# A fused attention and spectral mixing kernel: PV with v stationary, shared diagonal score blocks, products in column tiles, transfers in pairs, and a new fixed order

## The chip, the cores and the metric

The kernel runs on one core of one Trainium2 chip. The metric is the device time of one launch in microseconds (us), as the median of several runs. Each run also lists the mean clock that was granted to TensorE. A run is called slow here when it lies over 1.5% above the fastest run of the same kernel, and slow runs are left out of ratios. PE is TensorE (PEld its weight loads), DVE is VectorE, ACT is ScalarE, POOL is GpSimd, SP is SyncE, which issues the transfers.

## The reference, cut to what matters

```python
def _A_ref(x, wq, wk, wv, wo, beta):          # x: 1 x 2048 x 640, 32 heads of 20, 4 segments of 512
    ...
    for s in range(N):
        qs, ks, vs = (q[:, :, s].copy(), k[:, :, s].copy(), v[:, :, s].copy())
        logits = jnp.einsum('bhqd,bhkd->bhqk', qs, ks) * scale + mask     # causal inside the segment
        p = _softmax(logits, axis=-1)
        a_dot = jnp.einsum('bhqk,bhkd->bhqd', p, vs)
        pq = phi(qs)
        num = jnp.einsum('bhld,bhde->bhle', pq, M)                         # memory of earlier segments
        den = jnp.einsum('bhld,bhd->bhl', pq, z)[..., None] + 1e-06
        outs.append(g * num / den + (1.0 - g) * a_dot)
        pk = phi(ks)
        M = M + jnp.einsum('bhld,bhle->bhde', pk, vs)
        ...
    return o @ wo
def _B_ref(x, w_r, w_i):                       # irfft2(rfft2(x) * W)
    ...
return g * a + (1 - g) * b                     # g = sigmoid((x * gate_w).sum(-1))
```

## The kernel before

All work is recorded as operations with their dependences, and a fixed list, found by a search ahead of time, says in which order each engine runs them. The kernel computes a schedule from that list with an assumed duration for every operation. The schedule sets only the buffers and semaphores; the engines then run strictly in that order. The part of it that concerns the port shared by VectorE and POOL:

```python
def one(self, eng, fn, n, r, w, prio, per=None, fix=None, name="", after=()):
    fix0, per0, late = {"act": (65, 0.833, 110.0), "dve": (67, 1.04, 68.0), "pool": (100, 0.945, 50.0)}[eng]
    ...                                                     # assumed ns: fix + per * n
def head(e):                                                # when could engine e start its next operation?
    ...
    if e == "dve" and o.lock:                               # o.lock: needs the shared port
        t = max(t, free["pool"])                            # assumed to go when POOL's present instruction ends
    elif e == "pool":
        t = max(t, port)
```

Attention works on 32 groups (4 segments, 8 groups of 4 heads). For one group, scores come from row-tiled products (4 heads at a time, 20 rows each), exponentials on ACT, masks on POOL, and PV products that hold the exponentials stationary and stream 21 columns of v (20 and one of ones, which gives the denominator):

```python
UNITS = (((0, (0,)),), ((0, (1, 3)),), ((1, (0,)),), ((0, (2,)), (1, (2,))), ((1, (1, 3)),))
# exp: one activation for each unit, 4 heads x 512 columns; 80 of 128x2048 in all
self.one("act", lambda e: e.activation(dst(), src(), ACT.Exp, scale=SC), 4 * width, ...)
for g, j in outs:                                            # 4 masks a group, one for each diagonal block of 128
    self.one("pool", lambda e, g=g, j=j: e.affine_select(
        self.ex.ap(self.exo(s, g) + JOFF[j], [1280, 4], [1, P]), ...,
        [[0, 4], [1, P]], ALU.is_ge, 0.0, base=0, channel_multiplier=-1), 512, ...)
# pv_group: 4 tiles of queries x 4 heads x (i + 1) blocks = 40 products of 21 columns
return (self.ps(bank, i * 88 + hh * VW, [1, DH + 1]), self.ex.ap(...), va.ap(..., [1, DH + 1]), jj == 0, jj == i, {})
# then on VectorE: denominator * gate, reciprocal, multiplication, and an addition of the memory part
```

The softmax here doesn't subtract the row's maximum and nothing guards it: scores larger than these inputs give would overflow.

## Time and profile before

| | before |
|---|---|
| median of its first three runs | 246.75 us (246.59 to 250.73) |
| span of the profiled run | 244.2 us, clock 1.00 |
| POOL busy | 132.2 us, of which masks 81.0 |
| time the kernel's own schedule gives for its order | 238.5 us |
| changes between whole-array, row-tiled and column-tiled products | 175 |

The prediction shows the page's busy line, stretches of time and the chain. A line of the view of waits tells which engine and tile waited for which, the time in all, how often, and the longest wait. Two waits of the kernel before, those for masks and for scores:

```profile
ACT ex L1137 <- PE psum L498: 14.8, 36, 1.4
...
PEld psum L498 <- POOL ex L1140: 1.4, 5, 0.4
```

PE waited only 1.4 us for masks.

### The profile page before, as it was taken

To read this page: it belongs to the slowest core of one execution; us is meant where nothing else is said; L and a number is where in the kernel's file an instruction comes from. 1 tells how busy PE (TensorE), PEld (TensorE's weight loads), DVE (VectorE), ACT (ScalarE), POOL (GpSimd) and SP (SyncE) were. 2 spreads that over 40 slices of the span, in tenths; PEclk is the share of its full clock that TensorE was granted. 3 is DMA by queue.
4 is the path that set the end of the run, shared out by engine and by line. 5 is a ranking of instruction groups with operands and counts; after the bars stand their busy time and mean duration, and the time that the engine had idled before them with its cause. 6 is when DMAs were issued, how large, how long until landed. Compare 5 with 4: busy or idle time off the path is not lost.

```text
span 244.2 us, 8905 instructions
## 1 busy us (share of the span) xinstructions
PE 233.1 (95%) x3702; PEld 139.8 (57%) x3702; DVE 198.8 (81%) x534; ACT 201.6 (83%) x204; POOL 132.2 (54%) x200
## 2 busy tenths in 40 slices
PE   7999999999999999999978999999899999999994
PEld 2344575557556457645644475645555667667683
DVE  1489997988999898979999999989999975643643
ACT  2088889999998998999987998888899878798820
POOL 8421861362648484455876385646567656407610
PEclk9999999999999999999999999999999999999999
DMA  7998866696493656756442546313442969586224
GB/s 185 328 358 231 218 172 169 205 182 172 138 192 92 168 128 150 226 164 200 109 104 71 144 137 182 94 59 111 118 100 71 203 144 97 79 123 116 77 62 131
DMA packets 55880, 36.71 MB, mean 150 GB/s; under 512 B 31792, under 2 KB 52128, under 8 KB 55840
## 3 DMA queue, kind: packets, MB, share of 16 engines
q1 hardware_dynamic: 54144, 35.32, 58.4%
q10 hardware_dynamic: 1696, 0.82, 1.2%
q8 instruction: 29, 0.48, 0.8%
q14 instruction: 11, 0.09, 0.1%
HBM read 19.86 MB, written 9.71 MB: 121 GB/s over the span
## 4 chain that ended last, share of the span: by engine, by line
PE 72%; DVE 16%; DMA 5%; ACT 4%; issue 2%; SPq 0%; DVEq 0%
PE psum L498 64%; PE psum L496 8%; DVE Pt L1287 4%; ACT ex L1137 3%; DMA xT<-in_A_x_dram 2%; DMA oT<-o_scr 2%; DVE Cp L509 2%; DVE Yt L1292 1%; DVE qu L509 1%; ACT et L1010 1%; DVE va L1045 1%; DVE Bt L509 1%; DVE on L1172 1%; DVE on L1177 0%; DVE phk L1021 0%
## 5 line engine op out<-in xcount | busy, mean ns | idle before, releaser
L1137 ACT ACTIVATE ex<-psum 128x2048 bf16<-128x2048 f32 x80 | 150.3, 1878 | 15.8 <-PE psum L498 14.8
L1140 POOL TENSOR_SCALAR_AFFINE_SELECT ex<-ex 128x512 bf16<-128x512 bf16 x128 | 81.0, 653 | 70.5 <-ACT ex L1137 66.7
L498 PEld LDWEIGHTS psum<-va,ex 128*128 128x128 bf16 x1280 | 39.0, 96 | 5.8 <-issue 1.3
L498 PE MATMUL psum<-va,ex 128*128 128x21 bf16 x1280 | 41.1, 172 | 0.1
L498 PE MATMUL psum<-xT,wk 128*128 128x512 bf16 (+1 forms) x140 | 33.3, 380 | 0.6 <-DMA xT<-in_A_x_dram 0.6
L498 PE MATMUL psum<-xT,wq 128*128 128x512 bf16 (+1 forms) x135 | 32.2, 380 | 1.2 <-DVE Bt L509 1.2
L498 PE MATMUL psum<-qp,kp 20*128 20x384 bf16 (+3 forms) x512 | 31.7, 301 | 0.7 <-ACT ex L1137 0.2
L498 PE MATMUL psum<-wv,xT 128*128 128x500 bf16 (+1 forms) x160 | 31.9, 300 | 0.2
L1287 DVE TENSOR_TENSOR Pt<-psum,Wt 128x642 bf16<-128x642 f32 x32 | 25.4, 822 | 0.8 <-PE psum L498 0.5
L496 PE MATMUL psum<-wo,oT 128*32 128x320 bf16 x480 | 23.0, 300 | 0.2 <-issue 0.2
L498 PEld LDWEIGHTS psum<-qp,kp 20*128 20x128 bf16 x512 | 9.0, 92 | 18.3 <-ACT ex L1137 9.6
L509 DVE CAST ot<-psum 128x320 bf16<-128x320 f32 x21 | 9.9, 489 | 11.6 <-PE psum L496 8.4
L498 PEld LDWEIGHTS psum<-wv,xT 128*128 128x128 bf16 x160 | 13.3, 97 | 10.0 <-DVE Ac L509 0.8
L498 PE MATMUL psum<-big,Ac 128*128 128x321 bf16 (+2 forms) x96 | 17.9, 256 | 0.8 <-DVE Cp L509 0.4
L1045 DVE TENSOR_TENSOR va<-psum,ebx 128x500 bf16<-128x500 f32 (+1 forms) x32 | 15.2, 484 | 3.5 <-PE psum L498 2.8
L498 PE MATMUL psum<-tt,Yt 128*128 128x256 bf16 (+1 forms) x96 | 17.0, 274 | 0.4 <-DVE qu L509 0.2
L1292 POOL TENSOR_TENSOR Yt<-Pt 128x321 bf16<-128x321 bf16 x18 | 13.4, 757 | 7.2 <-DVE Pt L1287 4.6
L509 DVE CAST qu<-psum 128x512 bf16<-128x512 f32 x20 | 13.6, 686 | 3.4 <-PE psum L498 3.2
L1333 DVE TENSOR_TENSOR G<-eo,psum 128x320 bf16<-128x320 f32 x32 | 14.9, 479 | 1.7 <-PE psum L496 0.9
L498 PEld LDWEIGHTS psum<-xT,wk 128*128 128x128 bf16 (+1 forms) x140 | 9.9, 97 | 10.9 <-issue 2.3
L1177 POOL TENSOR_TENSOR on<-on,mem 128x320 bf16<-128x320 bf16 x16 | 12.8, 806 | 5.8 <-DVE on L1172 5.8
L1172 DVE TENSOR_TENSOR on<-psum,rs 128x320 bf16<-128x320 f32 x32 | 15.3, 481 | 0.6
(85 smaller groups left out, 379.9 us busy)
## 6 DMA issues: line engine op xcount, KB each, us to landing
tt<-tab_tt SPq DMA_DIRECT2D x16, 256.0 KB, 3.3
xsb<-in_A_x_dram SPq DMA_DIRECT2D x8, 320.0 KB
kp<-k_scr SPq DMA_DIRECT2D x28, 80.0 KB
qp<-q_scr SPq DMA_DIRECT2D x28, 80.0 KB
o_scr<-on SPq DMA_DIRECT2D x12, 160.0 KB
out_dram<-ot SPq DMA_DIRECT2D x12, 160.0 KB
q_scr<-qu SPq DMA_DIRECT2D x6, 256.0 KB
k_scr<-qu SPq DMA_DIRECT2D x6, 256.0 KB, 3.9
```

The costliest lines, as they stand in the source:

```text
L496: h = e.matmul(dst, wt, r_, start=st, stop=sp_, **{**kw, "tile_position": (0, q), "skip_group_check": True})
L498: h = e.matmul(o_, l_, r_, start=st, stop=sp_, **kw)
L509: alts["dve"] = (lambda e: e.tensor_copy(dst(), src()), 67 + 1.04 * n, 68.0)
L1010: self.one("act", lambda e: e.activation(et.ap(0, [1, L]), qsl(), ACT.Exp), L, [qb], [b("et", pi_)], late, name="phi_exp")
L1045: self.one("dve", lambda e: e.tensor_tensor(va.ap(i * H * VW + h0 * VW, [VW, nh], [1, DH]), self.ps(bank, 0, [DH, nh], [1, DH]), self.ebx. ...
L1137: self.one("act", lambda e: e.activation(dst(), src(), ACT.Exp, scale=SC), 4 * width, [bank], [self.exb(s, g, j) for g, j in outs], prio - ...
L1140: self.one("pool", lambda e, g=g, j=j: e.affine_select(self.ex.ap(self.exo(s, g) + JOFF[j], [1280, 4], [1, P]), self.ex.ap(self.exo(s, g) ...
L1172: self.one("dve", lambda e, rs=rs, bank=bank, g=g: e.tensor_tensor(on.ap(80 * g, [D, 4], [DH, 4], [1, DH]), self.ps(bank, 0, [88, 4], [VW, ...
L1177: self.either(lambda e, g=g: e.tensor_tensor(on.ap(80 * g, [D, 4], [1, 80]), on.ap(80 * g, [D, 4], [1, 80]), self.mem.ap(80 * g, [D, 4], [ ...
L1287: self.one("dve", lambda e, ri=ri, Pt=Pt, Wt=Wt, bank=bank: e.tensor_tensor(Pt.ap(ri * 322, [644, 2], [1, KD]), self.ps(bank, 0, [0, 2], [ ...
L1292: fn = lambda e, r=r, a0=a0, a1=a1, op=op, Pt=Pt, Yt=Yt: e.tensor_tensor(Yt.ap(r * 322, [1, KD]), Pt.ap(a0 * 322, [1, KD]), Pt.ap(a1 * 322 ...
L1333: self.one("dve", lambda e, q=q, n2=n2, bank=bank, eo=eo: e.tensor_tensor(self.G.ap(n2 * D + 639 * q, [1 - 2 * q, 320]), eo.ap(q, [1, 320] ...
```

## The change

Its intent is to relieve PE, ACT and DVE: PV products that stream wide instead of 21 columns, score blocks shared around the diagonal so that fewer columns are exponentiated, and a normalisation that goes through a scratch round trip for three of four segments. Masks become seven a group (three of 512 columns in all, four of 256). Some products of v move into column tiles, transfers are merged, and the order is searched anew. The core of the diff:

```diff
-JOFF = (0, 512, 1024, 896)
+KPOS = (0, 256, 128, 384)
+VPIECES = ((0, 0, 512, 0), (1, 512, 384, 128), (2, 896, 192, 320), (2, 1088, 64, 256), (3, 1152, 64, 448), (3, 1216, 64, 384))
...
+    def pv_flipped(self, s, g):
+        for n_, (jj, o, n, q0) in enumerate(VPIECES):
+            for hh in range(4):
+                    return (self.ps(bank, q0, [1, n], p0=32 * hh, np_=32), va.ap(jj * H * VW + (4 * g + hh) * VW, [1, 32]),
+                            self.ex.ap(self.exo(s, g) + hh * 1280 + o, [1, n]), n_ == 0, n_ == 5,
+                            {"tile_position": (0, 32 * hh), "skip_group_check": True})
...
-        for g, j in outs:
-            self.one("pool", lambda e, g=g, j=j: e.affine_select(...), 512, [], [self.exb(s, g, j)], prio, name="mask")
+            if ks == "a":
+                self.mask(s, g, P, 512, 0, 64, ("a0",), ("m1",), prio, 64)
+                self.mask(s, g, P, 0, 0, P, (), ("a0",), prio, 0)
+            elif ks == "b":
+                self.mask(s, g, 64, 512, 512, P, (), ("b0", "m1"), prio, -64)
+                self.mask(s, g, P, e2, e2, 64, (), ("b0" if s < 3 else "b1",), prio, 64)
+            else:
+                self.mask(s, g, P, 1216 if s < 3 else 1152, sh, 64, ("c0",), ("m3",), prio, 64)
+                self.mask(s, g, P, sh, sh, 64, (), ("c0",), prio, 0)
+                self.mask(s, g, 64, 1152, 1152, P, (), ("c0", "m3"), prio, ...)
...
-    ORDER = (36, 0, 86, 56, 38, ...)        # one entry for each operation and its engine
+    ORDER = (34, 0, 100, 54, 82, ...)
```

## The prediction

> **What bounds the kernel now.** I read part 1 of the page first, then the busy time by stretch, then the timelines of PE and ACT.
>
> ```profile
> PE 233.1 (95%) x3702; PEld 139.8 (57%) x3702; DVE 198.8 (81%) x534; ACT 201.6 (83%) x204; POOL 132.2 (54%) x200
> ```
>
> PE looks like the one bound, but its records contain pipeline latency. The timeline of PE gives the real pace from the start of one row to the start of the next:
>
> ```profile
> 77.77 1.15 PE L498 MATMUL psum<-va,ex 128*128 128x21 bf16 x40
> ...
> 236.53 2.35 PE L498 MATMUL psum<-wo,oTl 128*32 128x320 bf16 x64
> 238.71 0.31 PE L498 MATMUL psum<-G,fbg 128*32 128x320 bf16 x4
> ```
>
> Forty PV products take 1.15 us with one latency of about 0.15 in it: 25 ns each, for 21 columns. The 64 column-tiled products take 238.71 - 236.53 = 2.18 us, so a set of four, 320 columns wide, takes 136 ns, or 0.425 ns a column. At such paces (216 ns for 512 columns, 136 for 321, never under 25) all products of the trace stream for 203 us. There are 175 changes between whole-array, row-tiled and column-tiled products; from start to start, less streaming, a change costs about 0.09 us into a row-tiled score set, 0.13 to 0.17 out of it, and 0.20 from column-tiled to whole. At 0.13 on average that is 23 us. So PE needs about 226 of the 237 us after the first input lands at 7 us.
>
> ```profile
> 40.00:60.00 20.00, 20.00 (x241) 11.32 (x234) 16.60 (x43) 19.12 (x24) 8.19 (x14) 1.00 0.74 187
> 140.00:160.00 20.00, 19.87 (x304) 12.53 (x304) 18.81 (x58) 18.57 (x18) 12.97 (x20) 1.00 0.51 142
> 180.00:200.00 20.00, 19.25 (x371) 11.92 (x371) 18.61 (x56) 17.71 (x16) 14.28 (x20) 1.00 0.61 133
> 200.00:220.00 20.00, 19.79 (x532) 12.98 (x524) 10.37 (x26) 16.46 (x16) 7.20 (x12) 1.00 0.81 107
> ```
>
> The columns are PE, PEld, DVE, ACT, POOL busy, clock, DMA. From 20 to 200 us ACT and DVE are each over 90% busy, beside PE: three engines bound the middle together. After 200 us DVE is half idle and PE works off inverse transforms and output products. The chain that ended last agrees:
>
> ```profile
> PE 72%; DVE 16%; DMA 5%; ACT 4%; issue 2%; SPq 0%; DVEq 0%
> ```
>
> The change must therefore relieve PE, ACT and DVE together, or it moves the bound to the one left out. The groups it touches:
>
> ```profile
> L1137 ACT ACTIVATE ex<-psum 128x2048 bf16<-128x2048 f32 x80 | 150.3, 1878 | 15.8 <-PE psum L498 14.8
> L1140 POOL TENSOR_SCALAR_AFFINE_SELECT ex<-ex 128x512 bf16<-128x512 bf16 x128 | 81.0, 653 | 70.5 <-ACT ex L1137 66.7 <-ACT gate L1043 3.5
> L1172 DVE TENSOR_TENSOR on<-psum,rs 128x320 bf16<-128x320 f32 x32 | 15.3, 481 | 0.6
> L1170 DVE RECIPROCAL rs<-rs 128x16 f32<-128x16 f32 x32 | 7.8, 244 | 0.5
> L1167 DVE TENSOR_TENSOR rs<-psum,gate 128x16 f32<-128x16 f32 x32 | 5.4, 168 | 7.1 <-PE psum L498 6.7
> ```
>
> **What the Trainium skill says.** "TensorE: Matmul & The Clock Gate", section "Wait — 56ns, not 53.3ns?": starts of matmuls never come closer than about 25 ns, however narrow they are. The trace agrees: 25 ns for 21 columns, where streaming alone would be 9. "TensorEngine Tiling (Array Packing)", section "When to Use Tiling", names the cure used here: where the moving side is narrow, swap the operands and tile by columns. Its section "Key Properties" says that a change of tiling mode drains the engine; the trace agrees, at 0.09 to 0.20 us a change. "Perfetto Trace Analysis", section "Identifying the Most-Contended Engine", warns that matmul busy time is no measure of headroom for PE, while busy time is for ACT, DVE and POOL; 233 us of busy against 203 of streaming agrees.
>
> **The change part by part.**
>
> *PV with v stationary (24 of 32 head groups).* Removed: 40 products of 25 ns, 1.0 us a group. Added: six pieces of 512+384+192+64+64+64 = 1280 columns in four concurrent column tiles, 1280 x 0.425 = 0.544 us. Saved: 0.46 x 24 = 11.0 us of PE. Given back: the groups become column-tiled between row-tiled scores and whole-array products. The path whole, row, whole costs about 0.23 us, and whole, row, column, whole about 0.42, so 0.19 x 24 = 4.6 us. DVE loses 168 + 244 + 481 = 893 ns a group, 21.4 us of records, and about 3 us of additions of the memory part. ACT or DVE gains one eviction of 128x512 a group (599 ns on ACT, 686 on DVE): 24 x 0.64 = 15.4 us, shared. Normalization moves behind a scratch round trip: 15 multiplications of 128x512 (about 0.43 us from the equal-sized phk group, 6.5), 8 additions of 128x640 (0.5, 4) and 3 reciprocals of 128 columns (1 us each, an estimate from the 16-column one). All but the reciprocals fall in the last stage, where DVE is half idle.
>
> *Shared diagonal score blocks.* Score columns a group fall from 1280 to (1024 + 1024 + 256)/2 = 1152: 128 x 0.42 ns x 32 = 1.7 us of PE. Exponentials: ACT takes 1878 ns for 2048 columns and 599 for 512, so 0.833 ns a column plus 172. Segments 0 to 2: 48 of 2048 and 12 of 1024 (1025 ns) = 102.4 us. Segment 3, with split outputs: 8 of 2048, 8 each of 1280 (1238) and 768 (812), 8 of 512 = 36.2. Together 138.6 against 150.3: ACT saves 11.7, less 1.4 for eight more gate exponentials of 171 ns. Masks are dearer: seven a group, three of 512 columns (634 ns undisturbed) and four of 256 (375, an estimate from 634 and the 115 ns of a tiny memset): 3.4 us against 2.5, so 28 us more on POOL: 132 + 28 - 8 of removed additions = about 152 (62 to 65%). POOL has idle time for that, nearly all of it waiting for exponentials.
>
> *Few products in column tiles.* Half of the v projection becomes column-tiled with the same columns; eight visits at 0.27 us (into 0.08, out of it 0.20) cost 2 us unless they share a visit with PV. The transform products no longer follow a column-tiled neighbour: perhaps 1 us. K projections in two halves add 100 times 2.5 ns, nothing.
>
> *Transfers in pairs.* Fewer issues (pads 64 to 36, table loads 16 to 8, weights of the transform 66 to 32), against about 3 MB more written and 2 to 3 MB more read. With DMA share at 0.3 to 0.75 in the middle this is hidden; it matters at the end (0.81 at 200 to 220 us).
>
> *Order.* It can't be priced from the profile; I take it as about as good as the old one.
>
> *Sum.* PE: -11.0 - 1.7 + 4.6 + 2 + 1 = -5 us. ACT: -11.7 + 1.4 + half of the evictions (7.2) = -3. DVE: -21.4 - 3 + 3 + 8 = -13 before the last stage, +10 in it. ACT and DVE can trade evictions, so together they lose 16, or 8 each if balanced. The middle can shrink by 5 (PE, whose streaming and changes fill some 91% of the stretch from 70 to 200 us, so 9% of slack) to 8 (ACT and DVE). The last stage, bound by PE, keeps its output products; segment 3 gains only its exponentials. Together -7.5 us: 246.75 - 7.5 = about 239.
>
> **The rivals.**
> 1. *PE switching takes the gain.* If every PV set costs its own entry and exit (0.27 us), and v projections too, the saving on PE falls to 2 or 3 us and the time to 243. For it: changes are already 10% of the span. Against: the order was searched with their cost in it.
> 2. *POOL becomes the gate.* Seven masks per group in chains, all needed before a PV set starts; on top POOL shares additions with DVE. If PV sets wait, exponentials wait for their buffers and the time stays at 244 to 247. Against: before, PE waited only 1.4 us in total for masks.
> 3. *The end grows.* The round trip (store, gather, reciprocal, store, broadcast, multiply) lands in the last stage; the chain already has one 5.22 us stretch on a transposing load there. If it's late: 242 to 245. Against: segment 2 ends 50 us or more before the end.
> 4. *All waits fall too.* DVE sets the chain alone from 114 to 131 us, and PE's streaming falls to 61% there. With 13 us less on DVE, this hole could close: 232 to 235.
>
> **Range and chances.** The sum gives 239; rival 4 reaches down to 232, rivals 1 and 3 to 244.5. The threshold for faster is 241.8, so a loss of only a third of the sum makes it "within 2%". Three engines are relieved at once, which speaks for faster: 0.73; within 2%: 0.22; slower, if the order or POOL fails: 0.05.
>
> **What would show it.** Right: PV products of segments 0 to 2 near 0.55 us a group; about 200 or more changes of mode; exponentials at 138 to 139 us of ACT; POOL at 150 to 160 us; DVE near 195 us overall but lower before 190 us; PE still leading the chain. Wrong: mask waits of PE of several us; PE losing over 0.3 us around each PV set; a long DMA piece in the last 40 us; or a last stage longer than before, which would mean that the middle's gain wasn't carried to the end.

## The result, and the profile after

| | before | after |
|---|---|---|
| median, same rounds | 246.94 us (246.59 to 250.73, 4 runs) | 264.78 us (264.14 to 266.45, 4 runs) |
| span of the profiled run, clock | 244.2 us, 1.00 | 262.4 us, 0.98 |

The ratio of the times is 1.0738 (95% interval 1.0673 to 1.0803): the changed kernel is 7.4% slower, where 239.0 us was predicted. A ratio is the mean time of one kernel's fast runs over that of the other's of the same rounds, so not quite the ratio of the medians.

The busy line of the changed kernel's page and its chain by engine answer to the two that the prediction shows:

```profile
PE 232.3 (89%) x4352; PEld 143.5 (55%) x4367; DVE 215.5 (82%) x493; ACT 200.1 (76%) x237; POOL 169.2 (64%) x289
...
PE 40%; DVE 25%; ACT 11%; POOL 7%; issue 6%; DMA 5%; SPq 5%; DVEq 0%
```

POOL gained 37 us of busy time, and DVE, which was to lose some 4 us, gained 17. PE now leads 40% of the chain instead of 72%: something else holds it up. The groups of exponentials and masks (the columns are busy us, mean ns of one, idle time before and what ended it):

```profile
L1254 ACT ACTIVATE ex<-psum 128x2048 bf16<-128x2048 f32 (+4 forms) x92 | 138.6, 1507 | 26.1 <-PE psum L512 24.6
L1275 POOL TENSOR_SCALAR_AFFINE_SELECT ex<-ex 128x256 bf16<-128x256 bf16 (+2 forms) x224 | 123.0, 570 | 53.0 <-ACT ex L1254 50.2
```

The exponentials take the predicted 138.6 us to the digit, but ACT waits 24.6 us for scores instead of 14.8. The masks take 123.0 us instead of 81.0. By form:

```profile
L1275 POOL TENSOR_SCALAR_AFFINE_SELECT ex<-ex 128x256 bf16<-128x256 bf16 x128 | 60.6, 483 | 45.0 <-ACT ex L1254 43.7
L1275 POOL TENSOR_SCALAR_AFFINE_SELECT ex<-ex 64x512 bf16<-64x512 bf16 x64 | 43.8, 688 | 7.8 <-ACT ex L1254 6.5
L1275 POOL TENSOR_SCALAR_AFFINE_SELECT ex<-ex 128x512 bf16<-128x512 bf16 x32 | 21.9, 685 | 0.2
```

The narrow masks cost 483 ns, not the 375 of the prediction. Spans of POOL are rough, so I also took the time from start to start of masks that follow each other at once: its median is 421 ns for 256 columns and 624 for 512, so half the columns cost two thirds of the time. The kernel's schedule assumed 342 and 584 ns. In the kernel before, masks of 512 columns start 587 ns apart: each of the changed kernel's 96 wide masks takes some 37 ns more, about 4 of the 42 us. Its comparison has one more level in its pattern, which may be the reason. The waits of the changed kernel:

```profile
ACT ex L1254 <- PE psum L512: 24.6, 38, 4.3
PEld psum L512 <- POOL ex L1275: 10.1, 18, 2.8
...
PE psum L512 <- DVE mem L1151: 3.8, 1, 3.8
```

PE's waits for masks rose from 1.4 to 10.1 us. The last line is a wait for DVE; the timeline around it (start, duration, engine, line, operation) shows where it comes from:

```profile
184.14 3.37 POOL L1517 TENSOR_TENSOR oU<-oU,r 128x512 bf16<-128x512 bf16 x3
184.19 4.46 DVE L991 CAST omh<-gg 128x8 bf16<-128x8 f32 x1
...
187.47 1.15 POOL L1013 TENSOR_TENSOR fbg<-fcat,gbc 128x512 bf16<-128x512 bf16 x1
...
188.56 0.24 DVE L1146 RECIPROCAL dn<-dn 128x16 f32<-128x16 f32 x1
188.84 0.49 DVE L1151 TENSOR_TENSOR mem<-psum,dn 128x320 bf16<-128x320 f32 x1
...
189.38 0.72 PE L512 MATMUL psum<-big,Cp 128*128 128x321 bf16 x2 [3.77 <-DVE mem L1151]
```

A cast of eight columns takes 4.46 us. It starts 0.05 us after POOL began, and ends when POOL has run four instructions back to back. The next two DVE instructions come late, and PE idles for 3.77 us. The Trainium skill ("SBUF — State Buffer", section "Who interferes with whom") says that VectorE and GpSimd share a pair of ports as an exclusive lock, casts and `tensor_scalar` among the operations that can take it, and that the one that comes second waits until the first finishes. The trace fits this, and shows more than the page says: the cast lasted through four POOL instructions, not one. The prediction did not look at this page; it should have.

The cast is the worst case, not the only one. A group that the kernel's schedule marks as needing the shared port, DVE minima with both inputs in SBUF, in the kernel before and then in the changed kernel:

```profile
L1022 DVE TENSOR_TENSOR phq<-phq,et 128x512 bf16<-128x512 bf16 x15 | 6.5, 430 | 0.1
```

```profile
L1076 DVE TENSOR_TENSOR phq<-phq,et 128x512 bf16<-128x512 bf16 x15 | 8.9, 595 | 0.0
```

To count all, I compared each DVE instruction with the shortest of its own line and form; what it takes longer is called its excess here. The sum of the excess is 25.0 us before and 39.4 after; those longer by over 0.25 us are 18 (8.7 us) and 39 (23.4 us). POOL's runs of over 4 us without a gap of 0.15 us are 6 before (32 us in all) and 19 after (125 us, the longest 11.1 us).

The stretches of time (PE, PEld, DVE, ACT, POOL busy, clock, DMA share, GB/s) of the changed kernel show that the loss comes in bursts; the last two rows are cut finer, right after PE's two longest gaps:

```profile
100.00:120.00 20.00, 15.70 (x278) 8.54 (x277) 17.61 (x36) 16.72 (x21) 14.28 (x26) 0.94 0.75 153
...
140.00:160.00 20.00, 18.31 (x341) 10.13 (x340) 17.81 (x32) 16.87 (x19) 16.54 (x32) 1.00 0.63 181
...
180.00:200.00 20.00, 15.54 (x210) 8.06 (x211) 17.32 (x44) 12.19 (x15) 11.93 (x17) 0.83 0.52 131
...
117.50:120.80 3.30, 3.30 (x36) 2.01 (x34) 2.34 (x7) 2.72 (x4) 0.00 (x0) 0.50 0.52 105
189.30:195.80 6.50, 6.42 (x61) 2.76 (x62) 4.62 (x12) 3.34 (x3) 4.02 (x7) 0.50 0.66 114
```

PE's two longest idle gaps lie in the first and the third stretch (2.6 us at 113.8 us, 3.8 us at 185.6 us), and the granted clock is 0.94 and 0.83 there, 0.98 or more elsewhere. At a finer grain it is 0.50 for 3.4 us from 117.5 us and for 6.8 us from 189.2 us, shortly after each gap. That idleness lowers the clock is an argument from coincidence only. But the lowered clock can be part of the loss: 0.98 over a span of 262.4 us stands for at most some 5 us of PE's work at full clock (an estimate), and no experiment takes this part away by itself.

Against its own schedule the kernel falls behind in the same places. The table is worked out from the starts of ACT's operations in the trace, less the start that the kernel's schedule gives them, averaged over 10 us of the schedule:

| schedule's time from | before | after | after with masks cut short (masks_thin, below) |
|---|---|---|---|
| 50 us | 0.9 | 4.0 | 4.2 |
| 90 us | 1.4 | 7.3 | 5.4 |
| 110 us | 1.6 | 12.7 | 6.3 |
| 140 us | 4.0 | 15.6 | 8.0 |
| 170 us | 5.1 | 25.0 | 8.8 |
| 200 us | 5.2 | 27.6 | 10.0 |
| 220 us | 5.7 | 29.7 | 11.4 |

The two schedules end at 238.5 and 232.8 us. So the order was made for a gain of 5.7 us, near the 7.5 of the prediction, and lost 24 us more than the old one in being carried out.

### The profile page after: what moved, and what is told of

Read it like the earlier page. It is cut to its first block, busy times and chain, and to the rows that moved or that the text cites. A ratio compares the mean times of both kernels' runs of the same rounds, so it can differ in the third digit from the quotient of the medians.

```text
span 262.4 us, 10264 instructions
## 1 busy us (share of the span) xinstructions
PE 232.3 (89%) x4352; PEld 143.5 (55%) x4367; DVE 215.5 (82%) x493; ACT 200.1 (76%) x237; POOL 169.2 (64%) x289
## 4 chain that ended last, share of the span: by engine, by line
PE 40%; DVE 25%; ACT 11%; POOL 7%; issue 6%; DMA 5%; SPq 5%; DVEq 0%
PE psum L512 34%; ACT ex L1254 9%; PE psum L510 6%; POOL ex L1275 6%; DVE Pt L1430 3%; SPq L542 3%; DMA xsb<-in_A_x_dram 3%; DMA qkp<-qk_scr 3%; SPq L540 2%; DVE omh L991 2%; DVE xsb L897 2%; DVE Yt L1435 1%; DVE xf L892 1%; DVE qu L523 1%; DVE Bt L523 1%
## 5 line engine op out<-in xcount | busy, mean ns | idle before, releaser
L1254 ACT ACTIVATE ex<-psum 128x2048 bf16<-128x2048 f32 (+4 forms) x92 | 138.6, 1507 | 26.1 <-PE psum L512 24.6
L1275 POOL TENSOR_SCALAR_AFFINE_SELECT ex<-ex 128x256 bf16<-128x256 bf16 (+2 forms) x224 | 123.0, 570 | 53.0 <-ACT ex L1254 50.2
L512 PE MATMUL psum<-qkp 20*64 20x64 bf16 (+5 forms) x1280 | 33.0, 274 | 2.4 <-DMA qkp<-qk_scr 1.3
L512 PE MATMUL psum<-xT,wk 128*128 128x256 bf16 (+1 forms) x280 | 33.2, 273 | 0.7 <-DVE va L1106 0.7
L512 PE MATMUL psum<-wv,xT 128*32 128x320 bf16 (+3 forms) x400 | 30.3, 302 | 0.3 <-DVE Bt L523 0.2
L512 PE MATMUL psum<-big,Cp 128*128 128x321 bf16 (+1 forms) x96 | 19.3, 334 | 4.6 <-DVE mem L1151 3.8
L512 PE MATMUL psum<-ex,va 128*32 128x64 bf16 (+3 forms) x576 | 17.6, 257 | 6.4 <-DVE omh L991 2.6
L510 PE MATMUL psum<-wo,oU 128*32 128x320 bf16 x480 | 21.2, 300 | 1.7 <-issue 1.7
L512 PE MATMUL psum<-big,Ac 128*128 128x161 bf16 (+2 forms) x96 | 18.2, 258 | 0.5 <-DVE ub L523 0.4
L1063 ACT ACTIVATE et<-qu 128x512 bf16<-128x512 bf16 x25 | 15.5, 625 | 0.7 <-DVE phq L1076 0.6
## 6 DMA issues: line engine op xcount, KB each, us to landing
qk_scr<-qu SPq DMA_DIRECT2D x12, 256.0 KB, 3.8
u_scr<-ub SPq DMA_DIRECT2D x12, 256.0 KB, 3.3
```

Of the source, the lines that this page charges most:

```text
L510: h = e.matmul(dst, wt, r_, start=st, stop=sp_, **{**kw, "tile_position": (0, q), "skip_group_check": True})
L512: h = e.matmul(o_, l_, r_, start=st, stop=sp_, **kw)
L1063: self.one("act", lambda e: e.activation(et.ap(0, [1, L]), qsl(), ACT.Exp), L, [qb], [b("et", pi_)], late, name="phi_exp")
L1254: self.one("act", lambda e, d=d, q=q: e.activation(self.ex.ap(*d), self.ps(bank, *q), ACT.Exp, scale=SC), n, [bank], [self.exb(s, 2 * pr + ...
L1275: self.one("pool", lambda e: e.affine_select(self.ex.ap(e0 + d0, [1280, 4], [1, n], np_=np_), self.ex.ap(e0 + s0, [1280, 4], [1, n], np_=np_),
```

## The experiments

The theory: masks that are longer and more numerous than the order was made for delay PV sets, and POOL, always busy, starves DVE on the shared port. Rivals: PE loses its saving to changes of tiling mode; the new order is bad whatever POOL does; transfers are late. Sixteen kernels ran, in four calls; each is compared with the kernel before in the same call, whose medians there were 246.97, 247.10, 246.50 and 248.38 us. The changed kernel itself wasn't run again, so what an experiment gains is read here from the fast runs, as the difference of two ratios times 247 us; the whole loss is 18 us.

### 1. Masks nearly taken away: masks_thin

The masks are cut to 32 columns each after the first three groups. The result is wrong (relative error 0.051).

```diff
+        w = n if 8 * s + g < self.NEX else 8
-            self.ex.ap(e0 + d0, [1280, 4], [1, n], np_=np_), ...
+            self.ex.ap(e0 + d0, [1280, 4], [1, w], np_=np_), ...
```

> The changed kernel with its order kept, and every causal mask after the first three head groups cut to 32 columns (wrong output on purpose; the number of instructions, their order and their waits stay). Theory POOL: the masks (123.0 us against 81.0 before) are what delays the kernel; with some 90 us of them gone the time falls to 238 to 246 us. Rival TRANSFERS (the start and the merged transfers are late): at most 5 us are won, 259 us or more. Rival PE (more mode changes, 227 against 175): at most 3 us, 261 us or more.

Measured: 246.23 us (245.03 to 247.56), ratio to the kernel before 0.9986 (0.9932 to 1.004). The page's busy line and the wait for masks:

```profile
PE 228.0 (93%) x4367; PEld 141.5 (58%) x4367; DVE 195.6 (80%) x493; ACT 199.1 (82%) x237; POOL 107.9 (44%) x289
...
PEld psum L512 <- POOL ex L1276: 2.1, 7, 0.4
```

POOL lost 61 us of busy time, and the whole loss of 18 us is gone with it. DVE went from 215.5 to 195.6 us though none of its instructions changed: so 20 us of DVE's busy time were no work of its own. The order is the same, so the new order isn't what costs 18 us when masks are short. But 246 is not 239: a second question is left, taken up in 9 to 11.

### 2. Masks as long as the schedule assumed: masks_modelled

```diff
+        w = n if 8 * s + g < self.NEX else {64: 36, 128: 112}[n]
```

The columns go from 512 and 256 to 448 and 144, so that masks take about what the schedule assumed (570 and 328 ns from start to start in the trace, 14 less than the 584 and 342). The missing columns are wrong.

> The changed kernel with its order kept and each mask cut (wrong output on purpose) so that it takes about what the kernel's own schedule assumes: 448 instead of 512 columns (634 ns against 685 to 695 measured) and 144 instead of 256 (392 against 455 to 502). Theory MIS-SIZED MASKS: the order was searched with masks some 17 us too cheap in total, and each too long mask shifts all that follows; with the assumed lengths the time falls by 10 us or more, to 245 to 254. Rival: the size of the masks isn't the point, only their number, or nothing about them: 258 to 264.

Measured: 255.46 us (250.84 to 258.01), ratio of fast runs 1.0222 (1.0151 to 1.0293). The profiled run was slow (span 255.5 us), so only the length of its masks, above, is taken from it. Two of the four runs were slow, and the median holds them; the fast two took 253.40 and 250.84 us. By the fast runs about 13 us, some 70% of the loss, go with the extra length alone (by the median 9), what shorter masks take off the port included.

### 3. The DVE goes first: port_turns

Each DVE operation that the schedule marks as needing the shared port, and each small gate operation (the cast above is one, which the schedule doesn't mark), makes the POOL operation that comes next in the fixed order wait for it, so that POOL pauses once and DVE gets in. Nothing else changes.

```diff
+            if e == "dve" and (o.lock or o.name in ("gate_ops", "den_gate")):
+                turn = o
+            elif e == "pool" and turn is not None:
+                o.dyn.append(turn)          # one more semaphore wait
+                turn = None
```

> The changed kernel with one addition: after each VectorE instruction that needs the SBUF port shared with POOL, and after each small gate instruction, the next POOL instruction in the assumed order waits for it, so that POOL can't run on in front of it. Theory PORT: VectorE instructions are starved while POOL runs back to back (a cast of 8 columns took 4.46 us at 184 us with three multiplications and a table of POOL beside it); VectorE's excess of 39 us over its own shortest times against 25 before falls, and the time falls by 5 to 10 us, to 254 to 259. Theory POOL: POOL's work stays the same and gets extra waits: 262 to 268.

Measured: 253.45 us (251.4 to 256.0), ratio 1.0248 (1.0188 to 1.0308), output right.

```profile
PE 233.4 (92%) x4367; PEld 143.2 (57%) x4367; DVE 201.7 (80%) x493; ACT 199.5 (79%) x237; POOL 167.3 (66%) x289
```

Adding waits made the kernel 12 us faster (11 by the medians), more than the 5 to 10 expected. DVE's busy time fell by 14 us and its excess from 39.4 to 27.3 us, with POOL's work unchanged. This is the cleanest evidence for starving: no instruction became cheaper, only whose turn it was.

### 4. Both together: turns_and_modelled

> Both corrections at once, in the order of the change: port turns, and masks cut to the length that the order was made for (wrong output on purpose in the masks). If the two are the whole loss and act apart (11.3 and 9.3 us when done alone), the sum of both is 20 us and the time 243 to 248, about the kernel before and the run with thin masks. If they are two views of one cause, no more is won than with the better one: 251 to 255.

```diff
+        w = n if 8 * s + g < self.NEX else {64: 36, 128: 112}[n]
+            elif e == "pool" and turn is not None:
+                o.dyn.append(turn)
```

This is experiments 2 and 3 in one kernel, with the schedule told of the turns too (the masks again wrong at a few columns). Measured: 248.48 us (247.22 to 251.31), ratio 1.006 (1.0011 to 1.011); its profiled run was slow and isn't used. By the fast runs the two parts gave 13 and 12 us singly; together they give 17 of the 18, so they overlap by some 8 us. That shorter masks also block the port for less time is the likely reason, not shown apart.

### 5. The same dose in the kernel before: before_long_masks

Three of four masks of the kernel before are made twice as wide; the output stays right, because the extra columns satisfy the condition.

```diff
+MW = (256, 256, 256, 128)
-                [[0, 4], [1, P]], ALU.is_ge, ...
+                [[0, 4], [1, MW[j]]], ALU.is_ge, ...
```

> The kernel before with its order kept and three of the four masks of a head group widened from 128 to 256 columns a head (harmless: later columns pass the comparison anyway, the output stays right). This adds some 3 x 32 x 0.4 = 39 us of mask time to POOL, about as much as the change adds (42 us). Theory POOL: the kernel before slows by 8 to 18 us, to 255 to 265. Rival (POOL has idle time for it, the loss lies in the other parts): 247 to 251.

Measured: 268.36 us (265.84 to 271.85), ratio of fast runs 1.0846 (1.0776 to 1.0917). Its profile, of a slow run, has the same marks:

```profile
PE 241.9 (90%) x3702; PEld 142.2 (53%) x3702; DVE 211.3 (78%) x534; ACT 203.8 (75%) x204; POOL 173.6 (64%) x200
...
PEld psum L499 <- POOL ex L1141: 10.5, 20, 0.9
```

Some 41 us more of POOL work, in a kernel with nothing else of the change, cost 21 us, more than the 8 to 18 expected. An engine at 54% had no slack to give: POOL's idle time lay between masks, waiting for the next exponentials, and each mask stands between an exponential and a PV set. The 21 us aren't that delay alone: DVE's busy time rose from 198.8 to 211.3 us and its excess from 25.0 to 38.1 us in the same profile, so part of them is the port again. This kernel with turns wasn't run, so the two aren't separated here.

### 6. Turns in the kernel before: before_turns

> The kernel before with port turns alone, its order kept. If starving of VectorE by POOL is a cost of the change (longer back-to-back runs of POOL), the kernel before gains little: 243 to 248. If turns help any kernel alike: 236 to 241.

```diff
+            elif e == "pool" and turn is not None:
+                o.dyn.append(turn)
```

The same edit as in 3, with the schedule told of it. Measured: 246.51 us (245.87 to 249.7), ratio 0.9961 (0.9867 to 1.0056). It makes no difference that could be told; this kernel has few long runs of POOL (6, against 19) to be starved by.

### 7. Turns once more, in another order: slack_reordered and slack_no_turns

For the changed kernel with turns, and masks priced as measured, I searched the order anew, with transfers assumed 1 us later than the schedule does and a few other durations lengthened. Then the same order ran without turns.

```diff
-            [self.exb(s, g, k) for k in wk], prio, name=f"mask{d0}" + "bc"[np_ == P])
+            [self.exb(s, g, k) for k in wk], prio, name=f"mask{d0}" + "bc"[np_ == P], per=0.82, fix=220)
-    ORDER = (34, 0, 100, ...)
+    ORDER = (...)                            # result of the search
```

> The changed kernel with turns and another new order, made with transfers assumed 1 us later than the schedule has them, transposing issues longer, and VectorE instructions on the shared port 40 ns longer: an order that doesn't count on early transfers. In turns_reordered the chain held DMA 13%, and times slipped by 3 us at 45 us and by 4 us after 205 us behind transfers. Theory ORDER: with this slack the change pays, 236 to 243, below the kernel before by 2 to 4%. Rival (POOL, ACT and VectorE hold it whatever the order): 246 to 250, as turns_reordered.

> The same order without the turns. If POOL running on in front of VectorE is a cost by itself, it is 3 to 10 us slower than slack_reordered. If turns only repaired the order of the change, the two are within 1%.

Measured: with turns 248.56 us (247.69 to 250.25), ratio 1.0089 (1.0036 to 1.0142); without 264.46 us (262.09 to 265.82), ratio 1.0715 (1.0646 to 1.0784). The busy lines with turns, then without:

```profile
PE 230.8 (93%) x4367; PEld 142.1 (57%) x4367; DVE 193.8 (78%) x493; ACT 199.5 (80%) x241; POOL 160.3 (65%) x285
```

```profile
PE 239.3 (91%) x4367; PEld 144.0 (55%) x4367; DVE 206.7 (79%) x493; ACT 200.0 (76%) x241; POOL 162.9 (62%) x285
```

Turns are worth 16 us here, more than the 3 to 10 expected, and again show in DVE's busy time (13 us). So the effect isn't a quirk of one order. Two things enlarge it: this order was searched with turns in it, so it is made for them; and the clock of the profiled runs was 0.993 with turns and 0.955 without, which stands for up to 10 us between the two (an estimate: span times the missing share, 1.7 and 11.8 us).

### 8. Another search and its control: turns_reordered and before_reordered

An earlier search of the same kind, without the later transfers, for the changed kernel; and for the kernel before as control. Both edits have this form:

```diff
+                o.dyn.append(turn)
-    ..., name="mask")
+    ..., name="mask", per=0.82, fix=...)     # 220 in the changed kernel, 180 in the control
-    ORDER = (...)
+    ORDER = (...)                            # result of the search
```

> The changed kernel with the port turns of the run before, the masks priced at what they measured (430 and 640 ns of occupancy in place of 342 and 584), and the order searched anew with these prices; all instructions stay the same. Theory ORDER (the masks only hurt because the order was made for cheaper ones): with an order made for the real ones the time falls below the kernel before, to 236 to 245. Theory POOL WORK (42 us more on POOL can't be placed at all): 248 to 256, near the run with turns alone (253.5).

> The control: the kernel before with turns and an order searched anew in the same way and for the same time as in turns_reordered. Theory ORDER: it gets a little from the search too, 241 to 247, and turns_reordered lies 1 to 3% below it. Rival (the search is worth more than the change): it lies at or below turns_reordered.

Measured: 248.16 us (244.8 to 252.37), ratio 0.9993 (0.9886 to 1.01); the control 252.89 us (251.7 to 254.72), ratio 1.0236 (1.0154 to 1.0318). The control for slack_reordered:

> The control: the kernel before with turns and an order made in the same way with the same slack. Expected 244 to 249, about the kernel before; if slack_reordered lies 2% or more below it, the change itself pays once its order fits, and the loss was the order's.

Measured: 250.27 us (249.31 to 250.98), ratio 1.0137 (1.0085 to 1.0189). My searches are worse than the one that made the kernel before, by 3 to 6 us, where the first control was expected at 241 to 247 us; and turns_reordered missed the 236 to 245 us of the theory that the order alone was at fault. With like searches on both sides the changed kernel stands 2.4% and 0.5% below its control (quotients of the ratios, so of fast runs), but not below the kernel before by more than noise.

### 9. The flipped PV alone: flip_reordered

Score blocks, masks and projections of v stay as before; PV is flipped, transfers are paired, and the order is searched with turns.

```diff
-VPIECES = ((0, 0, 512, 0), (1, 512, 384, 128), (2, 896, 192, 320), (2, 1088, 64, 256), (3, 1152, 64, 448), (3, 1216, 64, 384))
+JOFF = (0, 512, 1024, 896)
+VPIECES = ((0, 0, 512, 0), (1, 512, 384, 128), (2, 1024, 256, 256), (3, 896, 128, 384))
```

> The changed kernel with only PV flipped, the merged transfers and the late weights kept: score blocks, exponentials and the four masks a head group as in the kernel before, no permuted keys, no column-tiled v projection; turns, and an order searched anew in the same way. If flipped PV is the gain and the shared score blocks the loss: 238 to 243, below turns_reordered. If the shorter exponentials of the shared blocks carry the gain: 244 to 250, no better than before_reordered.

Measured: 249.21 us (248.35 to 250.35), ratio 1.0084 (1.0016 to 1.0151). With only four masks a group, and POOL as busy as before (128.8 us), the flip alone gains no more than the whole change: it is 1.5% faster than before_reordered, its control (1.0236), and not faster than the kernel before. How far the PE side of the sum holds is seen without a chip run, from starts of products in the traces. The trace of the changed kernel lacks 15 of its 4367 products, so that of masks_thin stands for it. I took each product's streaming at the pace that the prediction gives, and the time from start to start at each change of mode less that streaming.

| | before | masks_thin (same products as after, all recorded) |
|---|---|---|
| streaming of all products | 203.2 us | 191.8 us |
| changes of mode | 175 | 227 |
| a change, median: whole to row / row to whole | 0.095 / 0.172 us | 0.094 / 0.163 us |
| a change, median: column to row / row to column | 0.197 / 0.170 us | 0.194 / 0.256 us |
| a change, median: column to whole / whole to column | 0.197 / 0.076 us | 0.196 / 0.093 us |
| changes, each kind by its median | 24.5 us | 34.3 us |
| together | 227.7 us | 226.1 us |

The streaming fell by 11.4 us, near the 12.7 predicted, but 52 more changes took 9.8 us back, where the prediction's sum gave back 7.6 (4.6 + 2 + 1). PE gains 1.6 us by this reckoning, in which some waits may hide in the medians; with the lower quartiles the changes take 7.8 us back, and PE gains 3.6.

The table may also tell why masks_thin falls behind its own schedule. The schedule prices a change at 94 to 110 ns; against the medians that is 6.7 us too little for the kernel before and 11.2 us for masks_thin (estimates from the counts of each kind). They end 5.7 and 11.4 us behind their schedules. So 4.5 of the 5.7 us by which the new order is shorter on paper may be changes priced too low. No run shows this apart, and the close agreement may be luck, as PE isn't the bound everywhere.

### 10. A late transfer: thin_big_later

In the trace of masks_thin the pads of q and k land at 45.5 us instead of the schedule's 41.4, beside an 824 KB table. The table is issued 3.5 us later.

```diff
-        ... (load of the table) ... (store of q) ...      # in ORDER
+        ... (store of q) ... (load of the table) ...
```

> The thin-mask version of the changed kernel again (wrong on purpose, relative error near 0.05), with one transfer issued later: the 824 KB table of the transform goes out behind the next store of q, some 4 to 5 us later, which costs nothing in the kernel's own schedule. If this table's packets delay the pads of q and k (planned to land at 41.4 us, landed at 45.5), the first exponentials of segment 1's groups start 2 to 3 us earlier and the time falls from 246.2 to about 243.5 to 244.5. If the pads are late for their own sake (many small packets behind late stores), the time stays at 245.5 to 247.

Measured: 246.39 us (245.94 to 247.1), against 246.23 before; wrong as masks_thin. The first pieces of the chain for the pads, in masks_thin and then here:

```profile
38.60 6.94 DMA qkp<-qk_scr
```

```profile
37.77 6.36 DMA qkp<-qk_scr
```

The pads landed 1.4 us earlier (0.8 by an earlier issue, 0.6 by a faster landing), and at 50 us of the schedule the kernel lagged by 2.8 instead of 4.2 us. The end did not move: a gain at the start was given back later. At 170 us of the schedule the kernel lagged by 6.6 us (masks_thin 8.8), at 190 us by 9.5 (9.2). Where the gain was lost, the chain runs through the scratch round trip: a store of 5.48 us and a gather of 3.33 us, from 188 to 197 us. So taking 1.4 of the 4.1 us from the lateness of the pads is worth nothing by itself, and the round trip is the likely next limit (no run tries it): rival 3 of the prediction, in a kernel whose masks are out of the way.

### 11. Orders searched with measured prices: priced_reordered, priced_reordered_2, before_priced

The changes of mode were priced in the search at 0.10 to 0.22 us, masks, VectorE and transfers as measured.

```diff
-    COST = {(0, 1): 94.0, (0, 2): 94.0, (1, 0): 110.0, (1, 2): 110.0, (2, 0): 110.0, (2, 1): 94.0}
+    COST = {(0, 1): 105.0, (0, 2): 100.0, (1, 0): 170.0, (1, 2): 220.0, (2, 0): 180.0, (2, 1): 170.0}
```

> The changed kernel with turns on the shared port and an order searched anew with measured prices: masks 460 and 670 ns, VectorE instructions 15 to 55 ns longer, changes between kinds of products 0.10 to 0.22 us, transfers landing 0.6 us later. Own schedule 242.0 us without the extra for transfers, 211 changes of mode (227 before the search). Theory A, the gain exists and the order lost it: 242 to 245 us, that is 0.5 to 2 per cent faster than the kernel before. Theory B, the gain is cancelled by the masks and the changes of mode whatever the order: 246 to 249, as in the two earlier searched orders.

> The same as the run before it with the result of another seed of the search (own schedule 242.1 us, 207 changes of mode): a second draw, which shows how far the outcome hangs on one order. Theory A: 242 to 245.5 us; theory B: 246 to 249.

> Control: the kernel before with turns, the same measured prices and as long a search (own schedule 243.6 us, 169 changes of mode). If prices alone make the gain, it runs at 242 to 245 us, as fast as the changed kernel; if the change itself is worth something, it lies 1 to 3 us above it. The two earlier controls ran at 252.9 and 250.3, so 245 to 248 is my middle.

Measured: 253.59 us (249.38 to 255.33), ratio of fast runs 1.0129 (1.0031 to 1.0227); 249.02 us (248.44 to 253.96), ratio 1.0076 (1.0009 to 1.0143); the control 249.44 us (246.93 to 250.59), ratio 1.0068 (1.0006 to 1.0131). In this call the kernel before itself ranged from 245.92 to 249.86 us in 11 runs. Better prices made the outcome more like the schedule in one case (242.1 against a span of 247.2 us), but neither seed beat the kernel before, nor the control (by the ratios 0.1% and 0.6% above it). This speaks for theory B of the expectation: the gain is cancelled, not merely hidden by the order. It isn't proof; a better order than any that ran could exist, and over all searches the changed kernel stands between 2.4% below and 0.6% above its like-searched control.

## Why the prediction was wrong, point by point

**What held.** The exponentials took 138.6 us, to the digit. A flipped PV set takes 0.53 to 0.54 us from its first start to its last in 23 of 24 groups, near the predicted 0.544. The streaming of PE fell by 11.4 us (worked out in 9), where 11.0 and 1.7 were predicted. Changes of mode passed 200 (227). The scratch round trip of rival 3 is no main part of the loss: the slip table grows by 2 us after 200 us of the schedule, as against 18 between 90 and 170. It comes on the chain only when the masks are out of the way (experiment 10).

**The step that failed first: "POOL has idle time for that".** The prediction added 28 us to POOL and dismissed rival 2 with "before, PE waited only 1.4 us in total for masks". Its own sign of being wrong, "mask waits of PE of several us", came: 10.1 us. The masks came as +42 us, since the 256-column one took 483 ns, not 375; POOL was busy for 169 us, not 150 to 160. But a wrong size costs time only where there is no room for it. The idle time of POOL lay in waits for exponentials, in front of masks that a PV set needs, so it was latency and not spare room. Experiment 5 shows it in the kernel before: 41 us on a half idle engine cost 21 us (the port's part included). Experiment 2 puts the length beyond what the order assumed at about 13 us, the port's part again included.

**The step that was missing: the port between POOL and DVE.** The prediction has DVE near 195 us; it was 215.5. The sum priced DVE and POOL as independent. Experiment 3 shows 12 us of the time in this coupling, experiment 7 shows 16 in another order, each with what the lowered clock adds. Rival 2 named POOL as a gate, and expected 244 to 247; with the port unpriced, its figure was too small by 18 to 21.

**"Order: I take it as about as good as the old one."** The order was good on its own terms (232.8 us assumed) and poor on the chip, because its assumed durations missed the masks by 40 to 80 ns each (from start to start) and its rule for the port let DVE in after one POOL instruction, and left casts out of it. A fixed order has no way to give way when an operation is late; each delay is passed on.

**"PE: -11.0 - 1.7 + 4.6 + 2 + 1 = -5 us".** This term is part of why even without masks the kernel only equals the old one. The give-back of 7.6 us was 7.8 to 9.8 and the streaming fell by 11.4 instead of 12.7, so PE, which paces most of the chain, gained 1.6 to 3.6 us instead of 5. Rival 1 said "2 or 3 us" and 243 us; it was right on the term. The total also took 7.5 us where its own first bound, PE, gave 5, and so leaned on slack in PE. By this reckoning the two are 4 to 6 of the 7 us that masks_thin lacks; the round trip, in 10, is another candidate.

**What stays open.** Of the 18 us, 17 are accounted for by two causes that were tried singly and together; how much of each acts through the lowered clock isn't known. That the remaining gain of the change is small, between nothing and some 2%, rests on the PE reckoning, on four searched orders of the changed kernel with turns (248.2 to 253.6 us) and one of its flipped PV alone (249.2) against their controls, and on masks_thin; whether some order reaches 243 isn't settled. No version of the changed kernel with right output beat the kernel before: the best, turns_reordered at 248.16 us, has a ratio of 0.9993.

## What to carry to other kernels

Idle time of an engine is spare room only if it doesn't stand between a producer and a waiting consumer: ask whether the new work is on the way from one engine to the next, and add it in the kernel before if a change can't be tried alone. When work moves to POOL, price what it takes from VectorE, look for DVE instructions that are longer than the shortest of their kind, and leave POOL a gap where DVE needs the port: a wait added on POOL saved 12 and 16 us. A fixed order is only as good as the durations it was made with, so measure every new shape before searching.

## What the Trainium skill lacked or had wrong

- "SBUF — State Buffer", section "Who interferes with whom", says that the one that comes second waits until the first instruction finishes. A VectorE cast of eight columns waited here through four POOL instructions (4.46 us, otherwise 0.15 to 0.27 us); the page lacks that a back-to-back POOL stream can hold VectorE off for longer than one instruction, and that a semaphore wait on POOL eases it (DVE 215.5 to 201.7 us of busy time in port_turns).
- No page that I found gives the duration of `affine_select` on POOL: from start to start 421 ns for 256 columns and 624 for 512 (bf16), so about 0.22 us of fixed cost and 0.8 ns a column, an estimate from these two (a mask of 32 columns in masks_thin took 211 ns, less than its 243).
- "TensorEngine Tiling (Array Packing)", section "Key Properties", says that a change of tiling mode drains the engine but gives no figure: the medians here run from 0.08 us (whole to column) to 0.26 us (row to column), and 52 more of them cost 7.8 to 9.8 us.
